# Convolution weights turned by VectorE instead of loaded twice, and part of a softmax moved to the stores

## The chip, the cores and the metric

The kernel runs on one core of one Trainium2 chip, with float32 throughout. The metric is the device time of one execution in microseconds; the median of three runs is given where several are at hand. A profiled execution also has a span, from its first to its last instruction, which the profile divides up.

## What is computed

Eight sequences of 3584 tokens with 192 channels go through a dynamic convolution: each token and head has 7 weights of its own, made by a softmax, which mix the token and its 6 predecessors in the head's 24 channels. The result x (28672 tokens of 192) goes through a soft mixture of experts with 32 slots: a dispatch softmax over all tokens for each slot, 8 small networks on 4 slots each, and a combine softmax over the slots for each token.

```python
# convolution
w = np.exp(weight_gen - np.max(weight_gen, axis=-1, keepdims=True))
w = w / (np.sum(w, axis=-1, keepdims=True) + 1e-09)
out = np.einsum('bshk,bskhg->bshg', w, x_unf)      # x_unf: the last 7 tokens
# experts
logits = x @ phi
d = np.exp(logits - logits.max(0, keepdims=True))   # over tokens
d /= d.sum(0, keepdims=True) + 1e-09
slot_input = d.T @ x
h = np.maximum(slot_input[e] @ w1[e], 0.0); slot_out[e] = h @ w2[e]
c = np.exp(logits - logits.max(1, keepdims=True))   # over slots
c /= c.sum(1, keepdims=True) + 1e-09
return c @ slot_out
```

## The kernel before

**Tiles.** A batch is cut into 35 groups of 104 tokens, a group into 4 blocks of 26 tokens. Two groups are a *pair* (140 in all), two pairs a *slot* of the schedule (70), seven groups a *set of taps* (40). The tokens are unfolded by matmul: for a block and a half of the heads, a *band* matrix (32 rows for 26 tokens and their 6 predecessors, 26 columns, heads in partitions of 32) holds the exponentials of the 7 weights in a diagonal band, and TensorE multiplies it with the rows of x (`conv`, L228 to L239, tile `cv` in PSUM, three buffers). A column of ones beside the channels gives the sum of the weights, so the softmax is normalized afterwards: `conv_sum` on ScalarE (L247), `conv_inv` (L253) and `conv_out` (L258) on VectorE.

**From weights to bands.** The weights of a set are loaded twice in one tile `taps` of 2 x 392 values a partition: once by token (for the maxima), once already spread over the rows of the band (`loadw`, L177). The steps of a set are `tap_top` (VectorE, maximum over 7 weights, L184), `tap_spread` (GpSimd, the maxima laid out by residue of the token, with the tile `own`, L190), `tap_rows` (TensorE, a matmul with the banded matrix `near` brings each maximum to the 7 rows that need it, tile `pmx` in PSUM, L196), `tap_sub` (VectorE, L201), `tap_exp` (ScalarE, L204), and `band_make` (GpSimd, L213), which copies the exponentials through a mask into the band: two instructions for each half of a set.

**Unit steps.** Every four slots form a unit: TensorE turns the conv results (`xpose`, L272), multiplies with phi (`logits`, L301), a running maximum is kept (`top`, `newmax`, `newmax_out`, L308 to L330), the exponentials of the logits are taken and turned (`dexp` L334, `dturn` L346), and `dispatch` (L365) adds the unit into the slots' inputs. `save` (L314) keeps the turned logits in LT for the combine softmax.

**The combine softmax** `soft` (L73) works on a half batch (18 or 17 groups, 16 halves) in seven steps: maximum (VectorE, L78), subtraction (GpSimd, L80), exponential (ScalarE, L83), sum (VectorE, L86), addition of epsilon (ScalarE, L88), reciprocal (VectorE, L90), product (GpSimd, L92). The first EARLY = 13 halves are done within the conv loop, the other three while the experts are computed.

**Order of the work.** The start is written out by hand (L376 to L436). The loop over slots 1 to 69 isn't: each operation is entered with an engine, a cost, what it reads and writes, and sometimes a lateness or a due time (`op`, L480); a list scheduler (`model`, L635) keeps TensorE's and SP's orders as entered and chooses the order for VectorE, ScalarE and GpSimd by the latest possible start. The program then goes out in that one order, each engine executing its own in order. All loads and stores are issued from SP.

**Experts and stores.** After the loop come the experts (`hidden`, `outputs`, L757 to L822), then the stores: 24 parts in `out_order` (L862), each with a matmul of the combine weights `cT` with the experts' output (`rows`, L834), two copies from PSUM to SBUF, VectorE's and ScalarE's by turns (`leave`, L841), and a store each. After most parts VectorE turns a later half of LT into cT (`turn`, L455).

Of the kernel before, what the change touches and what calls it, by code (L numbers as in the profile page):

```python
# [17 lines left out]
T = 26  # L18
# [13 lines left out]
EARLY = 13  # L32
# [9 lines left out]
def conv_soft_moe(ctx, tc, xh, wh, phi, w1a, w1b, w2, out):  # L42
# [30 lines left out]
    def soft(pool, h, step):  # L73
        g0, n = HALVES[h]
        lt = LT[:, g0 : g0 + n, :]
        if step == 0:
            rms[h] = pool.tile([128, 18, 1], F32, tag="rm", name=f"rm{h}")[:, 0:n]
# [6 lines left out]
        elif step == 3:  # L84
            sm = sms[h] = pool.tile([128, 18, 1], F32, tag="sm", name=f"sm{h}")[:, 0:n]
            V.tensor_reduce(out=sm, in_=lt, axis=AX.X, op=ALU.add)  # L86
        elif step == 4:
            A.activation(sms[h], sms[h], AF.Identity, bias=eps[:, 0:1])  # L88
        elif step == 5:
            V.reciprocal(sms[h], sms[h])  # L90
# [13 lines left out]
    NTM, NCV, NTAP, NBAND = 2, 3, 4, 3  # L104
# [4 lines left out]
    taps = [fix.tile([128, 2, TAPS], F32, name=f"taps{i}") for i in range(NTAP)]  # L109
# [6 lines left out]

    pmx = ps_l.tile([128, 512], F32, name="pmx")
    topP = pmx[:, 0:TAPS].rearrange("p (q l) -> p q l", q=KT)
# [19 lines left out]
    V.memset(one, 1.0)  # L138
    V.memset(xbd[:, 0:2, 0], 0.0)
# [7 lines left out]
    G.affine_select(out=near, in_=near, compare_op=ALU.is_ge, fill=0.0, base=0,  # L147
                    pattern=[[1, 128]], channel_multiplier=-1)
    G.affine_select(out=near, in_=near, compare_op=ALU.is_ge, fill=0.0, base=KT - 1,
                    pattern=[[-1, 128]], channel_multiplier=1)  # L150
    mask = keep.tile([128, 1, 32], F32, name="mask")
    maskT = keep.tile([128, 1, 32], F32, name="maskT")
    mask2 = keep.tile([128, 32, 1], F32, name="mask2")
    own = keep.tile([128, KT, 1], F32, name="own")
# [26 lines left out]
    def tap_top(s):  # L181

        tops[s] = pa.tile([128, NBC, 1], F32, tag="top", name=f"top{s}")
        V.tensor_reduce(out=tops[s][:, :, 0], op=ALU.max, axis=AX.X,  # L184
                        in_=taps[s % NTAP][:, 0].rearrange("p (l k) -> p l k", k=KT))

    def tap_spread(s, eng=G):

        tops[s] = pa.tile([128, KT, NBC], F32, tag="spread", name=f"spread{s}"), tops[s]
        eng.tensor_tensor(out=tops[s][0], in0=own.to_broadcast([128, KT, NBC]),  # L190
                          in1=tops[s][1].rearrange("p l o -> p o l").to_broadcast([128, KT, NBC]),
                          op=ALU.mult)

    def tap_rows(s):

        P.matmul(pmx[:, 0:TAPS], near, tops[s][0].rearrange("p q l -> p (q l)"),  # L196
                 start=True, stop=True)

    def tap_sub(s):
        r = taps[s % NTAP][:, 1]  # L200
        V.tensor_tensor(out=r, in0=r, in1=pmx[:, 0:TAPS], op=ALU.subtract)  # L201

    def tap_exp(s):
        A.activation(taps[s % NTAP][:, 1], taps[s % NTAP][:, 1], AF.Exp)  # L204
# [163 lines left out]
    def rescale(u):  # L368
# [3 lines left out]
        else:  # L372
# [3 lines left out]
    loadw(0)  # L376
    loadw(1)
    loadx(0)
    loadx(1)
    loadw(2)  # L380
    V.tensor_reduce(out=own[:, :, 0], axis=AX.XY, op=ALU.add,
                    in_=ident.rearrange("p (h j) -> p h j", j=32)[:, :, 0 : 4 * KT]
                    .rearrange("p h (m q) -> p q h m", q=KT))
    tap_top(0)
    tap_spread(0, V)
    tap_rows(0)
    for q in range(4):
        r = slice(32 * q, 32 * q + 32)
        G.tensor_copy(mask[r, 0, :], near[r, r])
    V.transpose(maskT[:, 0], mask[:, 0])  # L390
    V.tensor_copy(mask2, maskT.rearrange("p o i -> p i o"))
    tap_top(1)
    G.memset(xbd[:, 2:4, 3], 0.0)
    A.copy(xbd[:, 2:4, 1], zero.unsqueeze(1).to_broadcast([128, 2, HBC * GX]))
    G.memset(xbd[:, 2:4, 0], 0.0)
    G.memset(xbd[:, 2:4, 2], 0.0)
    for h in (0, 1):
        G.memset(xbd[:, 4, h], 0.0)
    tap_sub(0)
    tap_exp(0)  # L400
    tap_spread(1, V)
    warm(1)
    tap_rows(1)
    band_make(0, 0, 8, V)
    tap_sub(1)
    tap_exp(1)
# [6 lines left out]
    band_make(0, 8, 16, V)  # L413
# [5 lines left out]
    band_make(0, 16, HB, V)  # L419
    loadx(4)  # L420
    loadw(4)
# [47 lines left out]
    rowed = {SGG * s // 4 - 4: s for s in range(4, NSG)}  # L469
    rowed.update({1: 2, 2: 3})  # L470
    assert sorted(rowed.values()) == list(range(2, NSG))
# [44 lines left out]
    for late, what in ((1.0, x_of(2)), (1.7, x_of(3)), (0.0, ("w", 2)), (1.0, ("w", 3)),  # L516
                       (4.0, ("w", 4 % NTAP)), (5.0, x_of(4)), (0.0, ("band", 1, 0)), (2.5, ("band", 1, 1)),
                       (2.5, ("r", 1))):
        op(SP, 0.0, [], [what], lambda: None, late=late)
    softs = {}  # L520
    for h in range(EARLY):
        softs.setdefault((sum(HALVES[h]) - 1) // (2 * UP), []).append(h)
    for k in range(1, SLOTS):
# [32 lines left out]
        if k - 1 in rowed:  # L556
            s = rowed[k - 1]
            op(VE, 0.5, [], ["pmx", ("r", s % NTAP)], tap_sub, s)
            op(AC, 0.5, [], [("r", s % NTAP)], tap_exp, s)
            for h, (lo, hi) in enumerate(((0, 14), (14, HB))):  # L560
                op(PO, 1.8, [("r", s % NTAP)], [band_of(s, h)], band_make, s, lo, hi)

        for s in range(NTAP + 1, NSG):
            if k == max(s - NTAP, (SGG * (s - NTAP - 2) + SGG - 1) // 4):
                op(SP, 0.4, [], [("w", s % NTAP), ("r", s % NTAP)], loadw, s, late=6.0)
# [9 lines left out]
        steps = [(xpose, a - 2), (xpose, b - 2)] + ([(tap_rows, rowed[k])] if k in rowed else [])  # L575
        if k == 1:
# [374 lines left out]
```

## Time and profile before

| quantity | value |
|---|---|
| time of three runs, us | 347.49, 342.79, 348.1 (median 347.49) |
| profiled execution: its own time, its span, us | 347.02, 345.3 |
| mean granted TensorE clock in it | 0.943 |
| start and first slots, us from the span's start | 0 to 20 |
| planned loop, then last units | 20 to 267 |
| experts | 267 to 282 |
| stores | 282 to 345 |
| moved by DMA, MB | 80.82 |

The span lies 1.7 us below the execution's own time. Engines in the profile: PE is TensorE's matmuls, PEld its weight loads, DVE is VectorE, ACT ScalarE, POOL GpSimd, SP the engine that issues DMAs. A group of instructions is named by its line in the kernel, engine, operation and the tiles that it writes and reads; the shapes follow as partitions x elements, then the count, the busy time in us, the mean of one in ns, and the idle time of the engine just before them. A waiting row names who waited, for whom, us in total, how many times, and the longest. A row of a timeline has its start and its length in us, then engine, line, operation and count. A row of the windows gives, behind the stretch and its length, each engine's busy us with its instruction count, the granted clock of TensorE, the DMA engines' share and GB/s.

### The profile page before, as it was taken

How to read it: one execution, taken by the hardware profiler on the slowest of the kernel's cores; microseconds unless marked ns; L12 is line 12 of the kernel's file. 1: busy time of each engine (PE TensorE's matmuls, PEld its weight loads, DVE VectorE, ACT ScalarE, POOL GpSimd, SP SyncE). 2: the span in 40 equal slices, each digit the busy share in tenths (PEclk: the TensorE clock that was granted, in tenths of full speed). 3: DMA queues.
4: the chain of work that ended last, by engine and by line, in shares of the span. 5: the costliest groups of instructions: out<-in, count | busy, mean ns of one | idle time of the engine just before them, and what ended most of it. 6: DMA issues, size and time to landing. Idle time of an engine off the chain costs nothing.

```text
span 345.3 us, 16352 instructions
## 1 busy us (share of the span) xinstructions
PE 306.8 (89%) x6896; PEld 222.2 (64%) x6896; DVE 249.9 (72%) x550; ACT 161.7 (47%) x428; POOL 198.8 (58%) x261
## 2 busy tenths in 40 slices
PE   8789999899999998999999999899997988799600
PEld 6567777687778876778778777678784952124100
DVE  7766877878788886897887868777864759965400
ACT  6535454455645654456445544454632237534300
POOL 8679648679489785868778568586601720000000
PEclk9999999999999999999999999999999999975555
DMA  6787788877877777677876867966589009999995
GB/s 197 215 260 196 214 223 196 246 205 221 215 217 228 211 235 189 199 207 205 241 210 176 237 173 204 260 172 180 154 307 364 6 2 398 395 403 399 395 404 204
DMA packets 33001, 80.82 MB, mean 234 GB/s; under 512 B 7072, under 2 KB 7456, under 8 KB 32928
## 3 DMA queue, kind: packets, MB, share of 16 engines
q1 hardware_dynamic: 32928, 79.77, 74.7%
q8 instruction: 55, 0.90, 1.2%
q14 instruction: 18, 0.15, 0.2%
HBM read 57.38 MB, written 22.36 MB: 231 GB/s over the span
## 4 chain that ended last, share of the span: by engine, by line
PE 58%; DMA 19%; DVE 9%; ACT 4%; issue 3%; SPq 2%; POOL 1%; DVEq 0%; ACTq 0%; POOLq 0%
PE cv L237 25%; PE pt L272 12%; DMA taps<-wh 8%; DMA out<-big 7%; PE pmx L196 6%; PE ls L301 6%; PE acb L365 5%; DMA big<-xh 4%; DVE big L841 3%; PE hpb L765 2%; PE so L786 2%; DVE cT L455 1%; DVE top L184 1%; SPq L174 1%; DVE tm L258 1%
## 5 line engine op out<-in xcount | busy, mean ns | idle before, releaser
L213 POOL TENSOR_TENSOR band<-taps,mask 128x588 f32<-128x588 f32 (+3 forms) x158 | 121.3, 798 | 31.9 <-ACT taps L204 23.1
L237 PE MATMUL cv<-big,band 128*26 128x100 f32 x4480 | 120.4, 252 | 6.2 <-POOL band L213 1.5
L237 PEld LDWEIGHTS cv<-big,band 128*26 128x26 f32 x4480 | 101.0, 128 | 36.4 <-issue 29.0
L258 DVE TENSOR_TENSOR tm<-cv,ws 128x384 f32<-128x384 f32 x140 | 72.9, 551 | 6.7 <-DVE ws L253 1.0
L277 ACT COPY cm<-pt 128x312 f32<-128x312 f32 x140 | 51.9, 423 | 44.5 <-PE pt L272 44.0
L247 ACT ACTIVATE ws<-cv,eps 128x16 f32<-128x16 f32 x140 | 37.7, 272 | 58.0 <-PE cv L237 46.2
L272 PE MATMUL pt<-ident,tm 122*128 122x122 f32 x420 | 59.2, 277 | 0.7 <-ACT cm L277 0.7
L272 PEld LDWEIGHTS pt<-ident,tm 122*128 122x128 f32 x420 | 43.4, 141 | 16.4 <-issue 9.9
L253 DVE RECIPROCAL ws<-ws 128x32 f32<-128x32 f32 x70 | 24.3, 348 | 29.9 <-ACT ws L247 29.4
L190 POOL TENSOR_TENSOR spread<-own,top 128x392 f32<-128x392 f32 x37 | 31.2, 843 | 24.3 <-DVE top L184 13.0
L834 PE MATMUL po<-cT,so 32*128 32x468 f32 (+3 forms) x256 | 38.1, 726 | 5.2 <-DVE big L841 4.5
L841 ACT COPY big<-po 128x936 f32<-128x936 f32 (+2 forms) x25 | 22.4, 902 | 27.1 <-PE po L834 15.2
L196 PE MATMUL pmx<-spread,near 128*128 128x392 f32 x80 | 33.7, 503 | 1.6 <-POOL spread L190 0.8
L841 DVE COPY big<-po 128x884 f32<-128x884 f32 (+2 forms) x24 | 25.4, 1071 | 12.8 <-DMA out<-big 10.5
L834 PEld LDWEIGHTS po<-cT,so 32*128 32x128 f32 (+1 forms) x256 | 12.4, 188 | 29.7 <-DVE big L841 23.1
L184 DVE TENSOR_REDUCE top<-taps 128x56 f32<-128x392 f32 x40 | 22.1, 551 | 12.3 <-DMA taps<-wh 11.2
L301 PE MATMUL ls<-cm,phi_sb 128*32 128x208 f32 (+1 forms) x576 | 29.5, 334 | 0.3 <-issue 0.3
L204 ACT ACTIVATE taps<-taps 128x392 f32<-128x392 f32 x40 | 21.0, 525 | 17.5 <-DVE taps L201 14.5
L365 PE MATMUL acb<-tm,dt 128*32 128x193 f32 x536 | 26.6, 328 | 0.7 <-DVE dt L346 0.4
L301 PEld LDWEIGHTS ls<-cm,phi_sb 128*32 128x32 f32 x576 | 19.9, 109 | 4.6 <-issue 0.6
L201 DVE TENSOR_TENSOR taps<-taps,pmx 128x392 f32<-128x392 f32 x40 | 22.1, 553 | 0.4 <-PE pmx L196 0.4
L92 POOL TENSOR_TENSOR LT<-LT,sm 128x576 f32<-128x576 f32 (+1 forms) x16 | 18.1, 1132 | 5.1 <-DVE sm L90 4.9
(113 smaller groups left out, 256.0 us busy)
## 6 DMA issues: line engine op xcount, KB each, us to landing
big<-xh SPq DMA_DIRECT2D x320, 87.5 KB, 3.9
taps<-wh SPq DMA_DIRECT2D x40, 392.0 KB, 4.6
out<-big SPq DMA_DIRECT2D x23, 468.0 KB, 6.5
out<-big SPq DMA_DIRECT2D x24, 442.0 KB, 6.4
big<-w SPq DMA_DIRECT2D x8, 768.0 KB, 6.9
w1a_sb<-w1a SPq DMA_DIRECT2D x16, 256.0 KB, 3.9
w1b_sb<-w1b SPq DMA_DIRECT2D x8, 256.0 KB, 3.7
out<-big SPq DMA_DIRECT2D x2, 234.0 KB, 2.4
```

Source lines behind the costliest of these rows:

```text
L190: eng.tensor_tensor(out=tops[s][0], in0=own.to_broadcast([128, KT, NBC]), in1=tops[s][1].rearrange("p l o -> p o l").to_broadcast([128, KT ...
L196: P.matmul(pmx[:, 0:TAPS], near, tops[s][0].rearrange("p q l -> p (q l)"), start=True, stop=True)
L213: eng.tensor_tensor(out=w[:, j : j + n, l].rearrange("p (a k) l -> p a k l", k=k), in0=r[:, 0:k].unsqueeze(1).to_broadcast([128, n // k, k ...
L237: P.matmul(cv[32 * blk : 32 * blk + T, o : o + 4 * GX], bands[s % NBAND][:, :, bc], xbd[:, j % NXH, :, b * GX : (b + 1) * GX], start=True, ...
L247: A.activation(wss[p // 2][:, p % 2], cvs[p % NCV][:, 0 : 16 * GX].rearrange("p (h w) -> p h w", w=GX)[:, :, GW:], AF.Identity, bias=eps[: ...
L258: V.tensor_tensor(out=tms[u % NTM][:, pr, 1 : 2 * D + 1].rearrange("p (h w) -> p h w", w=GW), in0=cv[:, :, 0:GW], in1=wss[p // 2][:, p % 2 ...
L272: P.transpose(pt[:, i, 0:TR], tm[0:TR, pr, 1 + 128 * i : 129 + 128 * i], ident[0:TR, 0:TR])
L277: copy(cms[u][:, pr].rearrange("p i b j -> p (i b) j"), pts.pop(p).rearrange("p i (b j) -> p (i b) j", j=32)[:, :, 0:T])
L301: P.matmul(lp[32 * blk : 32 * blk + 32, 0:n, par, 0:T], phi_sb[:, 2 * par + i, :], cm[:, 0:n, 1 if i else 2 * par, blk, :], start=(i == 0) ...
L365: P.matmul(ac[32 * q : 32 * q + 32], dt[:, g, :], tm[:, g // 2, o : o + D + 1], start=(g < 4), stop=(g + 4 >= 2 * n))
L834: P.matmul(po[dst : dst + hi - lo, at, 0 : n * T], so[32 * q : 32 * q + 32, lo:hi], cT[32 * q : 32 * q + 32, g0 : g0 + n, 0:T], start=True ...
L841: (V.tensor_copy if done[1] % 2 else A.copy)(ot.rearrange("p (q c) -> p q c", c=n * T), po[:, 0 : len(qs), 0 : n * T])
```

## The change

- The weights of a set are loaded once, half the bytes: 28 block-slots (7 groups of 4 blocks) lie on partitions, and on each partition the 2 x 28 x 7 weights of a head's tokens.
- `tap_top` takes the maxima there; `tap_sub` subtracts them on the same partitions, on GpSimd (in the start, for set 0, on VectorE). The spread and the matmul of maxima are gone, with `own`, `mask`, `maskT` and the PSUM bank of `pmx`; that bank becomes a fourth `cv`.
- `tap_exp` writes the exponentials, in two instructions of 196, by row and place into one of two new tiles `places`, whose other values were set to zero once. A new step `tap_turn` turns its 32x32 blocks on VectorE into `byrow`, from which `band_make` reads.
- EARLY goes from 13 to 5: the experts' stage does halves 5 to 7 in place of 13 to 15, and halves 8 to 15 are done in the stores, one step a part, each ahead of the part's matmuls and copies.
- In the start x is loaded ahead of set 1, the band of set 0 is cut into more slices with the turn of set 1 among them, and the load of set 4 moves into the planned order. Slots and due times of the taps' steps change in the planned order.

```diff
-EARLY = 13
+EARLY = 5
...
-    NTM, NCV, NTAP, NBAND = 2, 3, 4, 3
+    NTM, NCV, NTAP, NPL, NBAND = 2, 4, 4, 2, 3
...
+    LB, TJ = NBC // 2, 4 * KT
+    taps = [fix.tile([128, 2, TJ, KT], F32, name=f"taps{i}") for i in range(NTAP)]
+    RS = TJ + KT - 1
+    places = [fix.tile([128, 2, KT, RS], F32, name=f"places{i}") for i in range(NPL)]
+    byrow = [fix.tile([128, 2, KT, 32], F32, name=f"byrow{i}") for i in range(NPL)]
...
+    for t in places:
+        G.memset(t, 0.0)
...
     def tap_top(s):
+        tops[s] = pa.tile([128, 2 * TJ, 1], F32, tag="top", name=f"top{s}")
         V.tensor_reduce(out=tops[s][:, :, 0], op=ALU.max, axis=AX.X,
+                        in_=taps[s % NTAP].rearrange("p b j k -> p (b j) k"))
+    def tap_sub(s, eng=G):
+        r = taps[s % NTAP].rearrange("p b j k -> p (b j) k")
+        eng.tensor_tensor(out=r, in0=r, in1=tops.pop(s).to_broadcast([128, 2 * TJ, KT]),
+                          op=ALU.subtract)
     def tap_exp(s):
+        p = places[s % NPL]
+        for b in range(2):
+            o = p[:, b, 0, 0:1]
+            to = bass.AP(o.tensor, o.offset, [list(o.ap[0]), [KT, 4], [RS + 1, KT], [1, KT]])
+            A.activation(to, taps[s % NTAP][:, b].rearrange("p (a q) k -> p a q k", q=KT), AF.Exp)
+    def tap_turn(s):
+        V.transpose(byrow[s % NPL].rearrange("p b q l -> p (b q) l"),
+                    places[s % NPL].rearrange("p b q i -> p (b q) i")[:, :, 0:32])
     def band_make(s, lo=0, hi=HB, eng=G):
         l = slice(2 * lo, 2 * hi)
-        r = taps[s % NTAP][:, 1].rearrange("p (q l) -> p q l", q=KT)[:, :, l]
+        b = lo // (HB // 2)
+        r = byrow[s % NPL][:, b, :, 2 * lo - LB * b : 2 * hi - LB * b]
...
     loadw(0)
+    loadx(0)
     loadw(1)
-    loadx(0)
...
     tap_top(0)
+    tap_sub(0, V)
+    tap_exp(0)
...
+    tap_turn(0)
...
+    band_make(0, 0, 8, V)
+    tap_top(1)
     G.memset(xbd[:, 2:4, 0], 0.0)
+    tap_sub(1, G)
     G.memset(xbd[:, 2:4, 2], 0.0)
+    tap_exp(1)
...
+    band_make(0, 8, 14, V)
+    band_make(0, 14, 16, V)
+    tap_turn(1)
...
     conv_sum(0)
+    band_make(0, 16, 22, V)
     band_make(1, 0, 6)
...
+    band_make(0, 22, HB, V)
     loadx(4)
-    loadw(4)
...
+    made = {}
+    for s in range(2, NSG):
+        made.setdefault(max(1, (SGG * (s - NBAND) + SGG - 1) // 4), []).append(s)
...
-        if k - 1 in rowed:
-            s = rowed[k - 1]
-            op(VE, 0.5, [], ["pmx", ("r", s % NTAP)], tap_sub, s)
-            op(AC, 0.5, [], [("r", s % NTAP)], tap_exp, s)
+        for s in made.get(k, ()):
+            op(VE, 0.5, [("w", s % NTAP)], [("top", s % 2)], tap_top, s)
+            op(PO, 0.85, [("top", s % 2)], [("w", s % NTAP)], tap_sub, s)
+            op(AC, 0.75, [("w", s % NTAP)], [("pl", s % NPL)], tap_exp, s)
+            op(VE, 0.6, [("pl", s % NPL)], [("r", s % NPL)], tap_turn, s)
             for h, (lo, hi) in enumerate(((0, 14), (14, HB))):
+                op(PO, 1.8, [("r", s % NPL)], [band_of(s, h)], band_make, s, lo, hi)
+            if s - 1 + NTAP < NSG:
+                op(SP, 0.4, [], [("w", (s - 1) % NTAP)], loadw, s - 1 + NTAP, late=5.0)
...
-    for kind, b, st, parts in out_order():
+    making = {h + 3: 0, h + 4: 0, h + 5: 1, h + 6: 2, h + 7: 4, h + 8: 5, h + 9: 6, h + 10: 8}
+    for part, (kind, b, st, parts) in enumerate(out_order()):
+        for i, first in making.items():
+            if 0 <= part - first < 7:
+                soft(pc, i, part - first)
```

More of the change, by code (lines that the diff above doesn't have):

```diff
@@ L147, in conv_soft_moe @@
     G.affine_select(out=near, in_=near, compare_op=ALU.is_ge, fill=0.0, base=0,
+                    pattern=[[-1, 128]], channel_multiplier=1)
+    G.affine_select(out=near, in_=near, compare_op=ALU.is_ge, fill=0.0, base=KT - 1,
                     pattern=[[1, 128]], channel_multiplier=-1)
[L149 to L152, printed above, removed]
     mask2 = keep.tile([128, 32, 1], F32, name="mask2")
-    own = keep.tile([128, KT, 1], F32, name="own")
     sel4 = keep.tile([128, 4, NS], F32, name="sel4")
@@ L412, in conv_soft_moe @@
     conv_sum(0)
-    band_make(0, 8, 16, V)
+    band_make(0, 16, 22, V)
     band_make(1, 0, 6)
```

80 lines of the change are left out of this document (14 added, 66 removed).

## The prediction

> **What bounds the kernel now.** I read the page first: the shares of the engines and the chain that ended last.
>
> ```profile
> span 345.3 us, 16352 instructions
> PE 306.8 (89%) x6896; PEld 222.2 (64%) x6896; DVE 249.9 (72%) x550; ACT 161.7 (47%) x428; POOL 198.8 (58%) x261
> PE 58%; DMA 19%; DVE 9%; ACT 4%; issue 3%; SPq 2%; POOL 1%; DVEq 0%; ACTq 0%; POOLq 0%
> ```
>
> TensorE leads, but these are means over stages. So next the busy time by window: the planned conv loop (20 to 260 us), then two stretches of the stores.
>
> ```profile
> core 0: us, PE busy (x) PEld busy (x) DVE busy (x) ACT busy (x) POOL busy (x), PEclk, DMA share, GB/s
> 20.00:260.00 240.00, 232.03 (x5940) 181.39 (x5931) 189.68 (x449) 121.90 (x364) 172.80 (x212) 1.00 0.76 214
> 293.00:303.00 10.00, 7.57 (x72) 2.24 (x72) 9.63 (x12) 5.50 (x6) 0.00 (x0) 1.00 1.02 396
> 308.00:316.00 8.00, 8.00 (x38) 3.12 (x36) 4.28 (x5) 3.46 (x4) 0.00 (x0) 0.50 1.02 402
> ```
>
> In the loop TensorE has only 240.00 - 232.03 = 8.0 us without work, VectorE is at 79%, GpSimd at 72%, ScalarE at 51%. In the stores the DMA engines are full (share 1.02, about 400 GB/s) while VectorE is nearly full at first and then falls off, and GpSimd does nothing. The waits say who follows whom.
>
> ```profile
> ACT ws L247 <- PE cv L237: 46.2, 74, 2.1
> ACT cm L277 <- PE pt L272: 44.0, 51, 2.0
> DVE ws L253 <- ACT ws L247: 29.4, 46, 1.5
> POOL band L213 <- ACT taps L204: 23.1, 15, 4.2
> ```
>
> ScalarE waits for matmuls, VectorE waits for ScalarE. So the loop goes at TensorE's pace, and the stores at the pace of DMA. Everything that leaves TensorE's queue in the loop should come off the time; what enters the stores is free only as long as data stays ahead of the DMA.
>
> **Part 1: no matmul of maxima (L196).** Its price must be read from the spacing of TensorE's work, not from a record's length. First a slot with it, then one without:
>
> ```profile
> 139.21 1.61 PE L237 MATMUL cv<-big,band 128*26 128x100 f32 x64
> ...
> 140.75 0.85 PE L272 MATMUL pt<-ident,tm 122*128 122x122 f32 x6
> ...
> 141.43 0.83 PE L196 MATMUL pmx<-spread,near 128*128 128x392 f32 x2
> ...
> 142.19 1.60 PE L237 MATMUL cv<-big,band 128*26 128x100 f32 x64
> ...
> 145.13 0.84 PE L272 MATMUL pt<-ident,tm 122*128 122x122 f32 x6
> ...
> 145.91 0.91 PE L237 MATMUL cv<-big,band 128*26 128x100 f32 x32
> ...
> 153.72 0.48 PE L237 MATMUL cv<-big,band 128*26 128x100 f32 x12
> ```
>
> From transposes to conv: 142.19 - 140.75 = 1.44 us with the maxima, 145.91 - 145.13 = 0.78 without, so one costs 0.66 to 0.67 us. There are 40, one per set of taps. Four belong to the start, 36 to the loop: 36 x 0.67 = **-24.1 us**.
>
> **Part 2: the other engines in the loop.** Rows by form, the price of one last before the bar:
>
> ```profile
> L190 POOL TENSOR_TENSOR spread<-own,top 128x392 f32<-128x392 f32 x37 | 31.2, 843 | 24.3 <-DVE top L184 13.0 <-DMA big<-xh 4.2 <-PE acb L324 4.2
> L201 DVE TENSOR_TENSOR taps<-taps,pmx 128x392 f32<-128x392 f32 x40 | 22.1, 553 | 0.4 <-PE pmx L196 0.4
> L184 DVE TENSOR_REDUCE top<-taps 128x56 f32<-128x392 f32 x40 | 22.1, 551 | 12.3 <-DMA taps<-wh 11.2 <-POOL band L213 1.1
> L204 ACT ACTIVATE taps<-taps 128x392 f32<-128x392 f32 x40 | 21.0, 525 | 17.5 <-DVE taps L201 14.5 <-DMA big<-xh 2.8
> L314 DVE STREAM_TRANSPOSE LT<-ls 128x512 f32<-128x512 f32 x16 | 11.2, 702 | 0.0
> L314 DVE STREAM_TRANSPOSE LT<-ls 128x384 f32<-128x384 f32 x2 | 1.1, 558 | 0.0
> L83 ACT ACTIVATE LT<-LT 128x576 f32<-128x576 f32 x8 | 5.5, 688 | 0.7 <-POOL LT L80 0.7
> L80 POOL TENSOR_TENSOR LT<-LT,rm 128x576 f32<-128x576 f32 x8 | 9.3, 1161 | 0.0
> L86 DVE TENSOR_REDUCE sm<-LT 128x18 f32<-128x576 f32 x8 | 6.0, 746 | 0.0
> L88 ACT ACTIVATE sm<-sm,eps 128x18 f32<-128x18 f32 x8 | 2.5, 308 | 0.8 <-DVE sm L86 0.8
> L90 DVE RECIPROCAL sm<-sm 128x18 f32<-128x18 f32 x8 | 2.1, 262 | 1.7 <-ACT sm L88 1.5
> L213 POOL TENSOR_TENSOR band<-taps,mask 128x588 f32<-128x588 f32 x77 | 91.0, 1182 | 31.6 <-ACT taps L204 22.8 <-issue 8.1
> L213 POOL TENSOR_TENSOR band<-taps,mask 128x140 f32<-128x140 f32 x77 | 32.6, 423 | 0.0
> ```
>
> VectorE: the subtraction leaves, 36 x 0.553 = -19.9. The new turn moves 14 blocks of 32, 448 elements, half way between the 384 and 512 rows: 0.63, so 36 x 0.63 = +22.7. The reduction keeps its 392 elements. Eight halves of the combine softmax leave the loop, two reductions and a reciprocal each, 8 x (2 x 0.746 + 0.262) = -14.0. New sum 189.7 - 19.9 + 22.7 - 14.0 = 178.5 us, against 240.0 - 24.1 = 215.9 us of loop: 83%. GpSimd: the spread (0.843) leaves, a subtraction over as many elements comes, taken at the same price; the eight halves take 8 x 2 x 1.16 = 18.6 away, 154 us or 71%. ScalarE: one exponential of 392 becomes two of 196; from the 392 and 576 rows an element costs (688 - 525) / 184 = 0.89 ns, so one of 196 takes 0.35 us, and a set 0.70, +0.18 us on an engine that is half idle. None of the three reaches TensorE's pace, so these edits cost nothing themselves; TensorE's 215.9 us hide them. Without that cover the turn and the exponentials would cost 36 x (0.63 + 0.18), about 29 us.
>
> What is late next: a maxima matmul was also cover. It stood between the logits and the matmuls that wait for VectorE's running maximum and for the turned exponentials of a unit. Where it goes, these come sooner and VectorE is slightly fuller. Of 17 units perhaps half lose 0.2 to 0.3 us: **+2 us** of new TensorE gaps. From below: the fourth conv buffer in PSUM, and loads of half the bytes (392 KB to 196 KB a set), could take 2 us of the present 8 away. From above: rival 1. I take +2 since the spacing rows show TensorE never waiting long.
>
> **Part 3: the start.**
>
> ```profile
> 4.11 0.55 DVE L184 TENSOR_REDUCE top<-taps 128x56 f32<-128x392 f32 x1
> ...
> 7.77 0.66 DVE L213 TENSOR_TENSOR band<-taps,mask 128x336 f32<-128x336 f32 x2
> ...
> 8.56 0.92 PE L237 MATMUL cv<-big,band 128*26 128x100 f32 x32
> ```
>
> From maximum to first conv takes 4.45 us through spread, matmul, subtraction, exponential and band. The new chain is 0.55 + 0.55 + 0.70 + 0.63 + 0.66 = 3.1 us, with the 0.2 that conv trails the band 3.3: 1.1 earlier. But VectorE's queue now holds the turn of set 1, which waits for GpSimd's subtraction, itself behind memsets (two more for the new tile among them), and behind that turn stand the last band slices of set 0 (conv 2 waits for them). On GpSimd the bands of set 1 wait for the same turn. So I keep **-0.5 us**, between -2 and +2. Loads of x ahead of set 1 and a missing early load change only the order in SP's queue.
>
> **Part 4: the eight halves in the stores.** They add no DMA. They are put ahead of each part's copies, one step a part. GpSimd's 16 instructions lie on an idle engine, ScalarE's 8 x (0.69 + 0.31) on a half idle one. VectorE is the one that counts: its copies feed every second store.
>
> ```profile
> 284.82 1.04 DVE L841 COPY big<-po 128x884 f32<-128x884 f32 x1
> ...
> 285.79 0.72 DVE L455 STREAM_TRANSPOSE cT<-LT 128x544 f32<-128x544 f32 x1
> ...
> 286.44 1.09 DVE L841 COPY big<-po 128x936 f32<-128x936 f32 x1
> ...
> out<-big SPq DMA_DIRECT2D x23, 468.0 KB, 6.5
> out<-big SPq DMA_DIRECT2D x24, 442.0 KB, 6.4
> ```
>
> Start to start a copy takes 0.97 to 1.0, a turn 0.65 to 0.69. The stores hold 22.36 MB (with two of 234 KB), 55.9 us at 400 GB/s, 2.33 a part for 24 parts. VectorE needs up to 1.7 a part now, so DMA sets the pace. In the changed order the first nine parts hold 14 reductions (0.66 start to start) and 4 reciprocals (0.18): 10.0 us, with 8.6 of copies and 7 turns of 0.68 a total of 23.3, where DMA needs 9 x 2.33 = 21.0. VectorE sets the pace there and the DMA loses about 2.3 us, which it can't win back. From below 0, if VectorE's head start of some 2 us covers it; from above all 8 x (2 x 0.66 + 0.18) = 12.0. I take **+2.5 us**: a step a part gives each handoff over 2 us, more than the 1.16 of the longest step.
>
> **Sum.** The profiled execution took 347.0 us (span 345.3), 0.5 below the median of 347.5. 347.0 - 24.1 + 2 - 0.5 + 2.5 = 326.9, **327 us**.
>
> **Rivals.**
> 1. *TensorE's fullness is padding, and handoffs between the engines set the loop's pace.* Then the maxima only filled gaps, and what comes off is at most their weight loads, 12.2 us for 40 or 11.0 for 36:
>
> ```profile
> L196 PEld LDWEIGHTS pmx<-spread,near 128*128 128x128 f32 x80 | 12.2, 193 | 2.4 <-DVE spread L190 1.0 <-POOL spread L190 1.0 <-issue 0.4
> ```
>
> 347.0 - 11.0 - 0.5 + 2.5 = 338 us. For it: weight loads are busy for only 181.39 of 240 us. Against: ScalarE waits 90 us for TensorE. The Trainium skill (Trainium Kernel Development and Optimization, Performance Expectations) calls matmul busy time a bad metric and weight-load busy share a good one. By that rule the loop has 24% to spare, and the sum would be this 338; the waits in the trace do not agree. Chance 0.14, of which 0.04 over 340.
> 2. *The stores show all of the moved work:* +12.0 in place of +2.5, 336 us. For it: VectorE at 9.63 of 10 early in the stores. Against: half idle from 308 on. Chance 0.09, of which 0.03 over 340 with further waits.
> 3. *Slower: GpSimd's own order.* If it does a set's subtraction and then stands until exponential and turn are back, a set costs 0.84 + 0.70 + 0.63 + 3.2 for the bands = 5.4 us plus queueing. A set is 1.75 slots; four slots go from 139.21 to 153.72 in the timeline, 3.63 each, so a set has 6.35 us now. It decides from 0.95 us of queueing. With the 23.1 / 15 = 1.54 us of the POOL row: 6.94 x 37 sets is 22 us more than now, 347 + 22 + 2 = 371 us. Against: it now lays the next set's spread between the bands of this one. Chance 0.07.
> 4. *All present gaps go as well:* the fourth buffer and half the tap bytes take the 8.0 us away, 347.0 - 24.1 - 8.0 + 2 = 317 us. Chance 0.05.
>
> **How the numbers follow.** The forecast gets 0.65, its own range 320 to 333. Faster by over 2% (under 340; about what a measurement of this kernel tells from no change): 0.65 + 0.10 + 0.06 + 0.05 = 0.86; within 2%: 0.04 + 0.03 = 0.07; slower 0.07. The range goes from 319 (-24.1 - 2 - 2 + 0) to 338, which takes in rivals 1 and 2 at their prices.
>
> **What would show it.** Right: no line of maxima; four slots near 12.5 us (153.72 - 139.21 less three maxima); the loop with 8 to 12 us of TensorE gaps in it; VectorE at 80 to 85% of it; stores some 58 us with VectorE full for the first 20 and DMA share just under 1 there. Wrong: TensorE gaps of over 20 us in the loop, GpSimd idle behind the turn, DMA share under 0.8 in the first half of the stores, a turn over 0.8 us.

## The result and the profile after

Four runs of the changed kernel gave 332.66 to 339.14 us, median **333.18 us**; four runs of the kernel before on the same chip had a median of 346.05 us. The ratio is 0.9653, with a 95% interval from 0.9543 to 0.9763: 8 to 16 us faster, 12.9 by the medians. The forecast was 327 us, 20 less than the profiled execution of before. In the later runs the kernel before had medians from 341.96 to 342.71 us, so experiments are compared by their ratio to it in their own runs. The profiled execution of before, with 347.02 us, is one of the slow ones of its kernel, so lengths read from its profile lie a few us high. The profiled execution of the changed kernel took 332.66 us, with a span of 330.9. From its page, the span, the engines' shares, and the chain that ended last, by engine and by line:

```profile
span 330.9 us, 16312 instructions
PE 275.4 (83%) x6816; PEld 209.1 (63%) x6816; DVE 248.3 (75%) x549; ACT 165.4 (50%) x469; POOL 202.6 (61%) x265
PE 55%; DMA 14%; DVE 10%; POOL 7%; issue 5%; ACT 3%; SPq 1%; DVEq 0%; ACTq 0%; POOLq 0%
PE cv L238 25%; PE pt L273 12%; PE acb L366 6%; DMA out<-big 6%; PE ls L302 6%; POOL band L214 4%; DMA big<-xh 4%; DMA taps<-wh 4%; DVE big L828 2%; PE hpb L752 2%; PE so L773 2%; PE po L821 1%; POOL taps L190 1%; DVE sm L86 1%; SPq L175 1%
```

TensorE's busy time fell by 31 us, the span only by 14, and GpSimd and "issue" hold more of the chain (7% and 5%, for 1% and 3% before). Where the time came from is read from one tile, the sum `accS`, to which each unit adds once. Its view gives the first and last start of each form; first before, then after:

```profile
L371 DVE COPY accS<-acb x1: 324/324/324, 39.1 to 39.1; 128x193 f32<-128x193 f32 x1
L373 DVE SCALAR_TENSOR_TENSOR accS<-accS,al,cv x1: 417/417/417, 267.4 to 267.4; 128x193 f32<-128x193 f32 x1
```

```profile
L372 DVE COPY accS<-acb x1: 361/361/361, 38.6 to 38.6; 128x193 f32<-128x193 f32 x1
L374 DVE SCALAR_TENSOR_TENSOR accS<-accS,al,cv x1: 417/417/417, 252.2 to 252.2; 128x193 f32<-128x193 f32 x1
```

The copy is the first unit, the addition out of `cv` the last. The first comes 0.5 us sooner than before (38.6 against 39.1), the last 15.2 us sooner (252.2 against 267.4). From there to the end of the span it was 345.3 - 267.4 = 77.9 us and is 330.9 - 252.2 = 78.7: experts and stores lose 0.8. So the gain lies in the loop, from first to last unit 228.3 us before and 213.6 after. This length is compared over all kernels below. (The run e2 below has the loads and matmuls of before and took 342.78 us in its profiled execution; its loop is 224.7 us long, so the gain there is nearer 11 than 15.) Busy time by window, before from 20 us to the loop's end, then after: two windows of the start, the loop, and the end in three parts:

```profile
20.00:267.00 247.00, 237.44 (x6036) 184.87 (x6026) 192.75 (x456) 123.44 (x368) 174.14 (x216) 1.00 0.77 218
```

```profile
core 0: us, PE busy (x) PEld busy (x) DVE busy (x) ACT busy (x) POOL busy (x), PEclk, DMA share, GB/s
6.00:12.00 6.00, 2.39 (x78) 1.92 (x80) 4.72 (x18) 2.81 (x7) 5.64 (x6) 0.96 0.67 194
12.00:20.00 8.00, 6.84 (x162) 5.72 (x158) 4.44 (x10) 4.97 (x18) 6.30 (x19) 0.82 0.60 164
...
20.00:252.00 232.00, 214.69 (x5965) 175.90 (x5957) 182.33 (x432) 120.32 (x389) 159.25 (x202) 0.99 0.69 204
...
267.00:285.00 18.00, 12.63 (x88) 3.83 (x88) 18.00 (x29) 12.06 (x19) 10.88 (x10) 0.70 0.79 309
285.00:300.00 15.00, 10.46 (x91) 2.58 (x88) 14.91 (x23) 9.14 (x14) 6.94 (x7) 0.79 1.00 391
300.00:331.00 31.00, 9.13 (x88) 2.40 (x84) 10.56 (x11) 7.56 (x9) 0.00 (x0) 0.69 0.90 354
```

TensorE has 237.44 - 214.69 = 22.7 us less to do in the loop, about 34 matmuls of maxima at 0.67. But its idle time grew from 247.00 - 237.44 = 9.6 us to 232.00 - 214.69 = 17.3. Work taken away less gaps added, -22.7 + 7.7, is the 15 us of the loop. Who TensorE waits for there is spread thin (its longest waits for other engines and for loads, 20 to 252 us; the row of GpSimd is for the whole span):

```profile
PE acb L325 <- DVE mq L311: 3.3, 2, 2.8
PE cv L238 <- POOL band L214: 3.0, 4, 1.1
PE cv L238 <- DMA big<-xh: 2.1, 3, 1.6
```

```profile
POOL band L214 <- DVE byrow L203: 37.8, 23, 4.7
```

GpSimd's bands now wait 37.8 us for the turn, where they waited 23.1 for the exponentials; little of it reaches TensorE. The loads show a second difference. DMA issues with KB each and the median us from issue to landing, before and after:

```profile
big<-xh SPq DMA_DIRECT2D x320, 87.5 KB, 3.9
taps<-wh SPq DMA_DIRECT2D x40, 392.0 KB, 4.6
```

```profile
big<-xh SPq DMA_DIRECT2D x320, 87.5 KB, 3.2
taps<-wh SPq DMA_DIRECT2D x40, 196.0 KB, 3.3
```

The loads of x are the same in both kernels, and yet they land 0.7 us sooner beside taps of half the size.

### The profile page after: what moved, and what is told of

It is laid out like the page before. It is cut to its first block, busy times and chain, and to the rows that moved or that the text cites. A ratio compares the mean times of both kernels' runs of the same rounds, so it can differ in the third digit from the quotient of the medians.

```text
span 330.9 us, 16312 instructions
## 1 busy us (share of the span) xinstructions
PE 275.4 (83%) x6816; PEld 209.1 (63%) x6816; DVE 248.3 (75%) x549; ACT 165.4 (50%) x469; POOL 202.6 (61%) x265
## 4 chain that ended last, share of the span: by engine, by line
PE 55%; DMA 14%; DVE 10%; POOL 7%; issue 5%; ACT 3%; SPq 1%; DVEq 0%; ACTq 0%; POOLq 0%
PE cv L238 25%; PE pt L273 12%; PE acb L366 6%; DMA out<-big 6%; PE ls L302 6%; POOL band L214 4%; DMA big<-xh 4%; DMA taps<-wh 4%; DVE big L828 2%; PE hpb L752 2%; PE so L773 2%; PE po L821 1%; POOL taps L190 1%; DVE sm L86 1%; SPq L175 1%
## 5 line engine op out<-in xcount | busy, mean ns | idle before, releaser
L214 POOL TENSOR_TENSOR band<-byrow,mask 128x588 f32<-128x588 f32 (+3 forms) x158 | 120.7, 795 | 41.9 <-DVE byrow L203 37.8
L238 PEld LDWEIGHTS cv<-big,band 128*26 128x26 f32 x4480 | 103.1, 128 | 26.1 <-issue 16.7
L259 DVE TENSOR_TENSOR tm<-cv,ws 128x384 f32<-128x384 f32 x140 | 71.8, 551 | 6.2 <-DVE ws L254 0.9
L821 PE MATMUL po<-cT,so 32*128 32x468 f32 (+3 forms) x256 | 32.2, 713 | 12.0 <-DVE big L828 11.3
L190 POOL TENSOR_TENSOR taps<-taps,top 128x392 f32<-128x392 f32 x39 | 34.0, 877 | 10.1 <-DVE top L185 5.5
L821 PEld LDWEIGHTS po<-cT,so 32*128 32x128 f32 (+1 forms) x256 | 8.8, 185 | 34.9 <-DVE big L828 30.5
L366 PE MATMUL acb<-tm,dt 128*32 128x193 f32 x536 | 27.9, 340 | 2.0 <-DVE dt L347 1.5
L199 ACT ACTIVATE places<-taps 128x196 f32<-128x196 f32 x80 | 25.5, 378 | 3.9 <-POOL taps L190 3.7
L203 DVE STREAM_TRANSPOSE byrow<-places 128x448 f32<-128x448 f32 x40 | 25.2, 631 | 2.6 <-ACT places L199 1.5
L80 POOL TENSOR_TENSOR LT<-LT,rm 128x576 f32<-128x576 f32 (+1 forms) x16 | 18.0, 1131 | 10.7 <-DVE rm L78 10.7
(109 smaller groups left out, 224.4 us busy)
## 6 DMA issues: line engine op xcount, KB each, us to landing
big<-xh SPq DMA_DIRECT2D x320, 87.5 KB, 3.2
```

Of the source, the lines that this page charges most:

```text
L190: eng.tensor_tensor(out=r, in0=r, in1=tops.pop(s).to_broadcast([128, 2 * TJ, KT]), op=ALU.subtract)
L199: A.activation(to, taps[s % NTAP][:, b].rearrange("p (a q) k -> p a q k", q=KT), AF.Exp)
L214: eng.tensor_tensor(out=w[:, j : j + n, l].rearrange("p (a k) l -> p a k l", k=k), in0=r[:, 0:k].unsqueeze(1).to_broadcast([128, n // k, k ...
L238: P.matmul(cv[32 * blk : 32 * blk + T, o : o + 4 * GX], bands[s % NBAND][:, :, bc], xbd[:, j % NXH, :, b * GX : (b + 1) * GX], start=True, ...
L259: V.tensor_tensor(out=tms[u % NTM][:, pr, 1 : 2 * D + 1].rearrange("p (h w) -> p h w", w=GW), in0=cv[:, :, 0:GW], in1=wss[p // 2][:, p % 2 ...
L366: P.matmul(ac[32 * q : 32 * q + 32], dt[:, g, :], tm[:, g // 2, o : o + D + 1], start=(g < 4), stop=(g + 4 >= 2 * n))
```

## The experiments

Two theories stand against each other. **The matmuls:** the gain is the 24.1 us of TensorE that left, less new handoffs. **The loads:** TensorE's queue and the loads of x and taps held the loop at nearly the same pace, so that neither pays alone. The first four runs take the change apart.

### The matmuls of maxima alone (e1_no_rows)

On the kernel before; from the third set on, `tap_rows` returns ahead of its matmul, and the planner counts it as nothing.

```diff
     def tap_rows(s):
...
+        if s >= 2:
+            return
...
-            op(TE, 0.76, [("spread", i % 2)], ["pmx"], tap_rows, i)
+            op(TE, 0.0, [("spread", i % 2)], ["pmx"], tap_rows, i)
```

> The kernel before without the matmul of maxima from set 2 on (38 of 40 left out; the subtraction then uses the maxima of set 1; all else, the spread too, stays). My theory: TensorE sets the loop's pace and one such matmul costs 0.67 us, so 38 x 0.67 = 25 us less, minus a few us of gaps that open elsewhere: 347 to 322, up to 326. Rival 1 (fullness is padding): at most the weight loads, 12 us, so 335 or more.

Measured: 342.94 us against 342.71, ratio 0.9973 [0.9929, 1.0017]. The 24.1 us that were to come off are not there. Windows of 200 us in the loop, before and this kernel:

```profile
40.00:240.00 200.00, 195.49 (x4960) 152.34 (x4963) 160.88 (x379) 102.72 (x307) 149.92 (x184) 1.00 0.76 211
```

```profile
40.00:240.00 200.00, 186.02 (x5104) 153.32 (x5104) 165.26 (x392) 107.32 (x319) 156.04 (x191) 1.00 0.74 215
```

TensorE's idle time rises from 4.5 to 14.0 us in 200; the DMA engines move about as many GB/s as before (215 for 211). The profile can name only part of these gaps. The loads of x land hardly sooner (3.9 us before):

```profile
big<-xh SPq DMA_DIRECT2D x320, 87.5 KB, 3.7
```

### The moved halves alone, and the change without them (e2_moved_only, e3_early13)

The first is the kernel before with eight halves of the combine softmax in the stores; the second is the changed kernel with them back in the loop.

```diff
-EARLY = 13
+EARLY = 5
...
-            rms[h] = pool.tile([128, 18, 1], F32, tag="rm", name=f"rm{h}")[:, 0:n]
+            rms[h] = pool.tile([128, 18, 1], F32, tag="rm", name=f"rm{h}", bufs=4)[:, 0:n]
...
-    for kind, b, st, parts in out_order():
+    making = {h + 3: 0, h + 4: 0, h + 5: 1, h + 6: 2, h + 7: 4, h + 8: 5, h + 9: 6, h + 10: 8}
+    for part, (kind, b, st, parts) in enumerate(out_order()):
+        for i, first in making.items():
+            if 0 <= part - first < 7:
+                soft(pc, i, part - first)
```

> The kernel before with only the move of eight softmax halves into the stores. My theory: in the stores it costs 1 to 3 us, and the loop, paced by TensorE, gains less than 2 us from emptier VectorE and GpSimd queues: 345 to 349. Rival 2 (the stores show all of the moved work): plus 12, about 358.

```diff
-EARLY = 5
+EARLY = 13
...
-    making = {h + 3: 0, h + 4: 0, h + 5: 1, h + 6: 2, h + 7: 4, h + 8: 5, h + 9: 6, h + 10: 8}
+    making = {}
```

> The changed kernel with the eight halves put back into the loop (EARLY 13, none in the stores). If they add gaps in the fuller loop, the loop is 2 to 5 us longer and the stores about 1 us shorter: 334 to 338. If VectorE and GpSimd have room enough, the loop keeps its length and the time falls by that 1 us: 332.

Measured: 342.67 us, ratio 1.0011 [0.9975, 1.0046], and 331.37 us, ratio 0.9657 [0.9579, 0.9736] beside 0.9653 for the changed kernel. The move neither costs nor gains anything that can be measured in the whole time, on either side of the change.

### Both together (e6_no_rows_moved)

If VectorE at 80% were what held e1 back, moving its reductions out of the loop as well had to set the gain free. The edit is that of e1 with that of e2.

> As the first experiment, with the eight softmax halves moved to the stores as well. VectorE theory: 14 us less of VectorE in the loop lets it go faster, 330 to 335. Load theory: the loop stays at the pace of the loads, 341 to 344.

Measured: 343.53 us, ratio 0.9984 [0.9939, 1.0029]. Less work for VectorE in the loop sets nothing free; in the next run, e5, it is busier than in e1 (170.88 for 165.26 of 200 us), and the gain is there all the same.

### Half the bytes, with and without the matmuls (e5_no_rows_half, e9_half_only)

Both on the kernel before; from the fifth set on only the copy spread by rows is loaded. The first has the edit of e1 too.

```diff
-        SY.dma_start(taps[s % NTAP], wh[s])
+        if s < NTAP:
+            SY.dma_start(taps[s % NTAP], wh[s])
+        else:
+            SY.dma_start(taps[s % NTAP][:, 1], wh[s, :, 1])
```

> As the first experiment (no matmul of maxima from set 2 on), and from set 4 on only the second half of a set's bytes is loaded (the copy by token, which only the maxima need, is left out; 196 KB in place of 392). Load theory: in the first experiment the loop went from TensorE's pace to that of the loads of x, which queue behind the taps' bytes; with half of these gone it gains 8 to 12 us, 330 to 334. VectorE theory: VectorE and the three conv buffers set the pace as soon as TensorE is relieved, and bytes change nothing: 341 to 343.

> The kernel before with only the bytes halved from set 4 on (196 KB of taps in place of 392, the copy by token left out, so the maxima are those of an earlier set; the matmul of maxima stays). If TensorE and the loads both held the loop at nearly the same pace, this alone gives little: 338 to 342. If the loads alone set the pace, it gives what both together gave: 329 to 333.

Measured: 331.46 us without the matmuls, ratio **0.9602** [0.9522, 0.9682], and 336.77 us with them, ratio 0.9879 [0.9768, 0.9991], a gain between next to nothing and 2.3%. The windows of the two kernels, and the loads of x in the second:

```profile
40.00:240.00 200.00, 192.42 (x5323) 159.94 (x5312) 170.88 (x408) 111.33 (x333) 155.47 (x190) 1.00 0.69 204
```

```profile
40.00:240.00 200.00, 199.57 (x5216) 157.45 (x5212) 167.69 (x396) 107.50 (x321) 155.00 (x189) 1.00 0.65 187
```

```profile
big<-xh SPq DMA_DIRECT2D x320, 87.5 KB, 3.0
```

With half the bytes and the matmuls left in, TensorE has work for 199.57 of 200 us: here it is the bound, alone. Without the matmuls it is idle for 7.6 us, and the whole gain of the change is there, with no turn, no new `places`, no fourth `cv` and no moved softmax. The four kernels make a square: 1 (before), 0.997 (no matmuls), 0.988 (half the bytes), 0.960 (both). The two alone would multiply to 0.985; together they give 0.960, some 8 us more than the sum of their parts (by the medians of all runs 5.6 us more).

### The changed kernel with the old load (e8_after_twice)

The same from the other side: each set's taps lie twice in memory and are loaded twice over, in one transfer of 392 KB; nothing reads the second copy.

```diff
-    taps = [fix.tile([128, 2, TJ, KT], F32, name=f"taps{i}") for i in range(NTAP)]
+    tapd = [fix.tile([128, 2, 2, TJ, KT], F32, name=f"taps{i}") for i in range(NTAP)]
+    taps = [t[:, 0] for t in tapd]
...
-        SY.dma_start(taps[s % NTAP], wh[s])
+        SY.dma_start(tapd[s % NTAP], wh[s])
...
+    wh = np.stack([wh, wh], axis=2)
```

> The changed kernel with each set's taps loaded twice over in one transfer (392 KB as before; the second copy is read by nobody). Load theory: most of the gain is lost, 339 to 343. VectorE theory: 331 to 334 as the changed kernel.

Measured: 341.94 us against 342.41, ratio 0.9949 [0.9908, 0.9989]. Of the 3.5% that the change gained the bytes alone take 3.0 back; the issues and their order are those of the changed kernel. In the window and the loads:

```profile
40.00:240.00 200.00, 186.26 (x5113) 153.08 (x5110) 157.31 (x372) 105.21 (x341) 142.63 (x178) 0.98 0.73 215
```

```profile
big<-xh SPq DMA_DIRECT2D x320, 87.5 KB, 3.7
```

TensorE's idle time is 13.7 us, as in e1, and x lands at 3.7 us again. The waits of SP's queue (40 to 235 us) point at the place: by their releasers, SP holds back loads of x until taps have landed. Why an issue of x waits for taps, which it doesn't read, isn't shown. First this kernel, then before, then the changed kernel:

```profile
SPq L176 <- DMA taps<-wh: 12.7, 13, 1.7
```

```profile
SPq L174 <- DMA taps<-wh: 13.7, 16, 2.2
```

```profile
SPq L175 <- DMA taps<-wh: 0.3, 1, 0.3
```

### Another queue for the taps (e10_no_rows_act)

Is it only that x stands behind taps in SP's order? This is e1 with the loads of taps from the sixth set on issued by ScalarE.

```diff
-        SY.dma_start(taps[s % NTAP], wh[s])
+        (SY if s <= NTAP else A).dma_start(taps[s % NTAP], wh[s])
...
-                op(SP, 0.4, [], [("w", s % NTAP), ("r", s % NTAP)], loadw, s, late=6.0)
+                op(AC, 0.1, [], [("w", s % NTAP), ("r", s % NTAP)], loadw, s, late=6.0)
```

> As the first experiment (no matmul of maxima from set 2 on, 392 KB of taps a set), with the taps' loads from set 5 on issued from ScalarE's queue in place of SP's. If the bytes hold the x loads up because SP's queue stands behind them, x comes in time now: 330 to 335. If the 16 DMA engines themselves are too busy, the time stays at 339 to 343.

Measured: 345.06 us, ratio 1.0016 [0.9959, 1.0073]. Waits of SP for x itself have come up, and x lands no sooner:

```profile
SPq L174 <- DMA big<-xh: 11.5, 20, 1.1
```

```profile
big<-xh SPq DMA_DIRECT2D x320, 87.5 KB, 3.8
taps<-wh ACTq DMA_DIRECT2D x35, 392.0 KB, 4.6
```

So it isn't the order in SP's queue alone. What both queues share is left, the DMA engines or the memory behind them; which of these, no run shows. (ScalarE's own waits for x came with it, 5.1 us in 3 times, so this run tells less than e5 and e8.) The Trainium skill has a rule that fits (DMA: Bandwidth & Descriptors, Issuing engines are not separate DMA queues): transfers run on the same engines whoever issues them, and another issuer only saves issue time.

### What is still missing (e4_taps6, e7_after_cv3, e11_warm, e12_after_less_x)

All four are on the changed kernel. First, six tap buffers in place of four, so that taps are asked for earlier:

```diff
-    NTM, NCV, NTAP, NPL, NBAND = 2, 4, 4, 2, 3
+    NTM, NCV, NTAP, NPL, NBAND = 2, 4, 6, 2, 3
...
-    op(SP, 0.4, [], [("w", 0)], loadw, NTAP, late=4.0)
+    for s in range(4, NTAP + 1):
+        op(SP, 0.4, [], [("w", s % NTAP)], loadw, s, late=4.0)
```

> The changed kernel with six buffers for the taps in place of four, so that each set is requested two sets earlier. If the new TensorE gaps come from tap maxima that wait for late loads at the head of VectorE's queue (8.1 us in 6 waits in the changed kernel's profile), these waits vanish and 3 to 5 us go: 328 to 330. If the gaps come from the handoffs between GpSimd, ScalarE and VectorE (GpSimd waits 37.8 us for the turn), nothing changes: 333.

330.12 us, ratio 0.9662 [0.9599, 0.9724]: no change, though VectorE's maxima now wait 0.2 us for taps in place of the 8.1 in the changed kernel. Late taps are not what is missing. Then three `cv` buffers instead of four:

```diff
-    NTM, NCV, NTAP, NPL, NBAND = 2, 4, 4, 2, 3
+    NTM, NCV, NTAP, NPL, NBAND = 2, 3, 4, 2, 3
```

> The changed kernel with three conv buffers in PSUM as before. If the fourth buffer is what lets the loop go below TensorE's old pace, this is 338 to 342. If bytes or VectorE's load do, 331 to 334 as it is.

333.94 us, ratio 0.9756 [0.9715, 0.9798]. The fourth buffer may be worth 1%; the interval meets that of the changed kernel, so this isn't settled. Then the start, where TensorE's clock had dropped: more warming matmuls.

```diff
-WARM = 9, 5
+WARM = 9, 5, 5, 5
...
     conv(0)
+    warm(2)
     conv_sum(0)
...
     conv(1)
+    warm(3)
     conv_sum(1)
```

> The changed kernel with ten more idle matmuls in the start, five after each of the first two convs, where TensorE stands. If the half clock seen in the changed kernel's first 20 us (granted 0.82) costs time, 1.5 to 3 us go: 327 to 330 where the changed kernel stands at 331 to 332 on such a chip. If GpSimd's bands set the pace of the start, nothing: 331 to 332.

332.41 us, ratio 0.9737 [0.9642, 0.9833]: no gain. Its first windows:

```profile
6.00:12.00 6.00, 5.62 (x102) 4.94 (x105) 4.96 (x19) 3.06 (x7) 5.92 (x7) 1.00 0.68 206
12.00:20.00 8.00, 5.91 (x172) 4.75 (x164) 4.46 (x10) 5.07 (x19) 6.29 (x18) 1.00 0.66 181
```

The clock is 1.00 in both, to no effect that shows in the time; GpSimd is busy for 5.92 of 6 us and 6.29 of 8. It may be what paces the first slots; that was not tried by itself. Last, the loads of x: from the sixth tile of x on one quarter of each is left out.

```diff
-        for h in range(4):
+        for h in range(4 if j < NXH else 3):
```

> The changed kernel without a quarter of the loads of x (from the sixth tile of x on, the heads of the fourth 32 partitions are not loaded and keep old values): 7 MB and 75 issues fewer. If the loads of x still hold the changed kernel's loop, its TensorE gaps (10.9 us between 40 and 240 us) shrink to a few us and the time falls by 4 to 8 us, a ratio of 0.945 to 0.955 to the kernel before. If GpSimd's and VectorE's handoffs make the gaps, they stay, ratio 0.963 to 0.970.

319.65 us against 341.96, ratio **0.9351** [0.9306, 0.9395], 22.3 us below before. Its loop by window, and the loads of x:

```profile
20.00:238.00 218.00, 210.02 (x5949) 174.02 (x5949) 181.56 (x432) 120.09 (x388) 158.67 (x202) 0.99 0.62 186
```

```profile
big<-xh SPq DMA_DIRECT2D x245, 87.5 KB, 2.9
```

With 75 loads of 87.5 KB fewer, TensorE's idle time in the loop is 8.0 us in place of 17.3, and the loop from first to last unit is 202.8 us long in place of 213.6 (the table). Everything else of the change, the turn, GpSimd's waits for it and the other steps, is still in this kernel, and what they hold TensorE back is within those 8 us.

One rival stays beside the bytes: SP, which issues all loads in its order. In the changed kernel it issues eight loads of x in 4.46 us:

```profile
124.60 4.46 SPq L175 DMA_DIRECT2D big<-xh  x8
```

By this row all 320 would take SP some 178 us (an estimate) of the 230 from the first of them to the last (2.5 to 232.9 us). e12 leaves out 75 of these issues along with their bytes, and SP's waits for TensorE's convolutions to free a buffer of x grow (40 to 235 us), first the changed kernel, then e12:

```profile
SPq L175 <- PE cv L238: 8.8, 17, 1.5
```

```profile
SPq L175 <- PE cv L238: 35.7, 37, 2.2
```

All of SP's waits in that stretch of 195 us add up to 26.5 us in the changed kernel and 62.7 in e12, so in the first SP, too, has little room. For the taps the bytes decide (e8, e9); whether the bytes of x or SP's issuing of x hold the rest, e12 doesn't tell.

The length of the loop from first to last unit, in the profiled execution of each kernel (start of the copy, start of the last addition):

| kernel | taps a set | maxima in the loop | first, last unit, us | loop, us |
|---|---|---|---|---|
| before | 392 KB | yes | 39.1, 267.4 | 228.3 |
| e2, moved halves | 392 KB | yes | 37.7, 262.4 | 224.7 |
| e1 | 392 KB | no | 38.2, 264.3 | 226.1 |
| e6, e1 with moved halves | 392 KB | no | 39.0, 265.4 | 226.4 |
| e8, changed kernel, double load | 392 KB | no | 37.2, 261.6 | 224.4 |
| e10, e1 with taps from ScalarE | 392 KB | no | 38.7, 262.6 | 223.9 |
| e9 | 196 KB | yes | 36.9, 257.0 | 220.1 |
| e5 | 196 KB | no | 36.4, 247.4 | 211.0 |
| changed kernel | 196 KB | no | 38.6, 252.2 | 213.6 |
| e3, halves back | 196 KB | no | 36.6, 251.7 | 215.1 |
| e4, six tap buffers | 196 KB | no | 37.8, 250.0 | 212.2 |
| e7, three `cv` | 196 KB | no | 37.2, 253.9 | 216.7 |
| e11, warmed start | 196 KB | no | 36.9, 252.7 | 215.8 |
| e12, fewer loads of x | 196 KB | no | 35.4, 238.2 | 202.8 |

The rows fall into four groups, and the groups go by what is loaded: with full taps 224 to 228 us, whether the maxima are there or not; with half taps 220 with them and 211 to 217 without; with fewer loads of x as well, 203. Kernels with the same start (before and e2; changed, e3 and e7) reach the first unit up to 2 us apart, so a difference of that size in one execution means nothing.

From the last unit to the end of the span the same executions show what the moved halves cost. The six kernels that keep them in the loop (before, e1, e3, e5, e9, e10) take 77.8 to 77.9 us there, the eight that move them 78.4 to 78.8. So the move costs some 0.8 us at the end, too little to show in the whole time.

## Why the prediction was right, and where it was off

**Part 1, -24.1 us: the count and price held, the credit did not.** The row of maxima is gone. Four slots with only one stop, of 0.30 us, from the timeline of the changed kernel:

```profile
61.04 1.61 PE L238 MATMUL cv<-big,band 128*26 128x100 f32 x64
...
73.88 1.34 PE L238 MATMUL cv<-big,band 128*26 128x100 f32 x52
```

That is 12.84 us for 14.51 before; the forecast said near 12.5, which it is without the stop. 22.7 us of work left TensorE between 20 us and the loop's end. The step that failed is the reading ahead of it: "the loop goes at TensorE's pace", so that "everything that leaves TensorE's queue in the loop should come off the time". TensorE was 97.7% busy, and the work taken away alone gave 0.3% (e1). Even with half the bytes, taking the matmuls out shortens the loop by 9.1 us (220.1 in e9, 211.0 in e5) and not by 24.1.

That the forecast came as near as it did is luck. It asked for 20 us less and got 12.9; 333.18 lies just outside its own 320 to 333 and inside the whole range of 319 to 338. It got there only because the same change also halves the bytes, which it had counted at zero beyond a part of 2 us "from below"; with the bytes put back a gain of 0.5% is left (e8).

The sign of it stood in the profile. The forecast quoted the chain by engine, "DMA 19%", and took DMA for the stores' affair. The chain by line, one line further on the page of before, says otherwise:

```profile
PE cv L237 25%; PE pt L272 12%; DMA taps<-wh 8%; DMA out<-big 7%; PE pmx L196 6%; PE ls L301 6%; PE acb L365 5%; DMA big<-xh 4%; DVE big L841 3%; PE hpb L765 2%; PE so L786 2%; DVE cT L455 1%; DVE top L184 1%; SPq L174 1%; DVE tm L258 1%
```

Only 7% are stores; loads of taps and x hold 8 + 4 = 12%, 41 us, as much as the chain gives the transposes. The share isn't steady from one execution to the next: with the same loads e2's chain gives the taps 5%, so it is a sign and not a measure. In the half-bytes kernel with the matmuls (e9) the loads of x keep 1%, those of taps aren't on the line any more, and TensorE's lines have grown:

```profile
PE cv L240 32%; PE pt L275 15%; PE ls L304 8%; PE pmx L199 8%; PE acb L368 6%; DMA out<-big 6%; PE po L837 3%; DVE big L844 2%; PE hpb L768 2%; PE so L789 2%; DVE cT L458 1%; ACT big L844 1%; DMA big<-xh 1%; DVE spread L193 1%; DVE mask L394 1%
```

**New gaps, +2 us: mis-sized, 7.7 us.** The forecast asked for 8 to 12 us of gaps in the loop and called over 20 wrong; there are 17.3, where before had 9.6 and e2 6.7 (20 to 262 us). It looked for them in handoffs between engines. More than half go when loads of x are left out: with fewer of them (e12) they fall by 9.3 us, to 8.0, and the loop by 10.8. Not all of that was lost by the change, since the kernel before also gains some 4 us (1.2%) when its loads are eased (e9). What is left in e12, 8.0 us, need not be old: with lighter loads and the matmuls still in place (e9, 20 to 257 us) TensorE stands for only 3.5. So the new handoffs may account for some 4 us, an estimate across two kernels; no run takes them alone.

**Part 2, the other engines: right.** Turn, exponentials and subtraction in the changed kernel:

```profile
L190 POOL TENSOR_TENSOR taps<-taps,top 128x392 f32<-128x392 f32 x39 | 34.0, 877 | 10.1 <-DVE top L185 5.5
L199 ACT ACTIVATE places<-taps 128x196 f32<-128x196 f32 x80 | 25.5, 378 | 3.9 <-POOL taps L190 3.7
L203 DVE STREAM_TRANSPOSE byrow<-places 128x448 f32<-128x448 f32 x40 | 25.2, 631 | 2.6 <-ACT places L199 1.5
```

631 ns for the turn (0.63 forecast), 378 for an exponential (0.35), 877 for GpSimd's subtraction (0.84). VectorE is busy for 182.33 of 232 us, 79% (83 forecast), GpSimd for 69% (71). None of them became the bound.

**Part 3, -0.5 us: not told apart from nothing.** The first unit came 0.5 us sooner in the two profiles, as forecast, but the same start gives up to 2 us more or less from one execution to the next (the table).

**Part 4, +2.5 us: +0.8, the mechanism right.** VectorE is full for 18.00 and 14.91 us in the windows from 267 to 300, longer than the forecast 20. The DMA engines wait for it a little, as forecast: from 270 to 294 us they move 372 GB/s at a mean share of 0.95, where before, from 285 to 309, they move 400 at 1.02. That is some 1.7 us of stores by these rates (an estimate), of which 0.8 are left at the end, in every kernel with the move.

**The rivals.** Rival 1 (TensorE's fullness is padding, 338 us) was right in what e1 does: next to nothing came off. A part of TensorE's busy time was indeed padding: from first to last unit its records are busy for 220.98 us before (5617 matmuls) and for 216.84 in e9 (5618). But its cause, handoffs between engines, isn't what held e1 back, since the same handoffs are in e5; and its price was not met either, 11.0 us forecast and about 1 us measured. The Trainium skill's rule beside it (Trainium Kernel Development and Optimization, Performance Expectations), which distrusts matmul busy time, is borne out by e1; but once the loads were lighter, 199.57 of 200 us of that busy time were the bound (e9), so the rule didn't say what held the loop. Rival 2's stores did not come. Rival 3's wait came, 37.8 us of GpSimd behind the turn for 23.1 behind the exponentials, but GpSimd has the room, and TensorE waits only 3.0 us for its bands in the loop. Rival 4 (all gaps vanish) is the opposite of what happened.

## What to carry to other kernels

An engine that is 97% busy need not be the only bound, above all if the chain by line also holds a tenth of loads: take its work away in the trace and ask whether the bytes of the loop could come any faster, since the freed engine will ask for them sooner. When a change removes both work and bytes, the two may be worth more together than apart, as here; price each with the other left as it was. Read a load's pressure from its landing time and from the issuing queue's waits for earlier transfers, not from the mean share of the DMA engines alone, and count how much of the loop the issuing queue spends on issuing.

## What the runs showed of the hardware

**Loads paced a loop at a mean DMA share of 0.76.** The stores reach a share of 1.02 and 400 GB/s, the loop before only 0.76 and 211. Even so, taps of 392 KB instead of 196 put the landing of an 87.5 KB load of x from 3.0 to 3.2 up to 3.7 to 3.9 us (e9, e5 and after; e1, e8 and before), and took away the gain. The number of packets isn't the reason: it is 33001 before and 33000 in e9 and in the changed kernel, whose packets of taps are smaller. Whether an uneven load of the engines or the memory makes the delay was not tried; e12 lowers bytes, packets and issues together.

**The granted clock of TensorE fell without a long idle time.** In the changed kernel's start:

```profile
11.59 2.89 PE L238 MATMUL cv<-big,band 128*26 128x100 f32 x64 [0.80 <-DVE band L214]
```

```profile
8.90:12.30 3.40, 1.62 (x52) 1.48 (x56) 2.94 (x14) 2.15 (x6) 3.40 (x5) 0.88 0.54 163
12.30:15.70 3.40, 3.40 (x73) 2.95 (x67) 1.96 (x4) 0.51 (x3) 3.40 (x8) 0.62 0.49 131
...
32.80:36.20 3.40, 1.55 (x35) 1.31 (x38) 2.30 (x5) 0.31 (x2) 3.05 (x4) 0.88 0.76 192
36.20:39.60 3.40, 3.40 (x44) 2.33 (x40) 2.36 (x5) 0.54 (x3) 0.00 (x0) 0.62 0.63 182
```

64 conv matmuls take 2.89 us here and 1.61 later. Twice, a stretch in which TensorE was busy for under half of 3.4 us is followed by one with a mean clock of 0.62, though none of its idle times was over 1.8 us. It cost nothing here that could be measured: in e11 the clock stays at 1.00 in both places, and the time is no shorter.
